# A three-operation bit join cut to two: where the weights' low three bits are made, and which engine subtracts in the MLP's first block

## The chip, the core and the metric

The kernel is one program on one core of a Trainium2 chip. The core's engines are PE (TensorE, matrix products), DVE (VectorE), ACT (ScalarE), POOL (GpSimd) and SP (SyncE, which here only starts transfers). The metric is the device time of one launch in microseconds.

## The reference

Three layers follow each other; all results are float32.

```python
# 1. linear attention: q, k, v of (4, 8, 576, 64), w_phi of (64, 128)
proj = x @ w_phi; proj -= max|proj|; phi = [exp(proj), exp(-proj)]
kv = sum_s k_p[s] v[s];  z = sum_s k_p[s];  out = (q_p @ kv) / (q_p @ z + 1e-6)
# 2. MLP: 2304 tokens, 512 wide, 1536 hidden
xn = x / rms(x) * rms_g
y = (silu(xn @ w_gate) * (xn @ w_val)) @ w_out
# 3. soft mixture of 8 experts with 4 slots each
logits = y @ phi; d = softmax over tokens; c = softmax over slots
out = c @ (relu((d.T @ y) @ w1) @ w2)
```

The three MLP weights arrive as 64-bit floats. The kernel has to turn them into 32-bit floats itself, from the two 32-bit words of each number.

## The kernel before

The first stage (0 to 136 us) works through the keys in 18 tiles of 128 tokens. Per tile, PE makes two projections `P` (L392), one for each half of the heads, in a PSUM buffer each; DVE takes the largest absolute value `mx` (L396) and subtracts it, giving `pr` (L400); ACT makes two exponentials `kp` (L413, L414) for each half; PE adds up the sums over tokens `kacc` (L437, L446). Beside this runs the attention of the first 384 queries: projections `P` (L320), `qmx` and `qpr` on DVE (L323, L324), transposes `T` and their exponentials `e` (L335, L337), then for each of four pairs of heads the products `num` and `den` (L204, L212), a reciprocal on DVE (L217), eight small copies on ACT (L222) and a product `xraw` on DVE (L223). The PSUM buffers of `num`, `den`, `T` and L320's `P` are three in all, taken in turn.

The second stage is the MLP in six blocks of 384 tokens. Block 0 runs from 136 to 232 us. For each of 12 pieces `m` of 128 hidden units PE multiplies 12 times for the gate `pg` and 12 times for the value `pv` (both L795) and 9 times for the output `acc` (L820 to L822). Between them stand ACT's tanh `t` (L802), two DVE products (L803, L807), ACT's rounded copy `hh` (L101) and the remainder `hl` = t - hh (L104). L822 reads `hl`. In block 0 the attention of the next 384 queries is spread over the same steps.

The weights are converted in 18 pieces of 128 x 1024 numbers, nine in the first stage (one per two tiles) and nine in block 0 (one per `m`). A piece goes through: a transfer into `wraw` (L122, 1 MB); ACT's scaling of the high word, as a float, into `wt` (L126); three DVE operations on the bits of `wt` in place (L133 shifts left by 3, L135 joins the sign, L137 joins the upper three bits of the low word); ACT's rounded copy into the weight tile (L101); POOL's remainder (L104, the "parts"). `wraw` has three buffers in the first stage and two in block 0; a new transfer into one waits until the last join of the old piece has read it. `wt` has two buffers in turn, free after POOL's parts.

The pieces of conversion are called at fixed steps of the loops (`conv_join` and others), but the order on each engine is then set by a scheduler of the language, which has its own estimates of durations. So the order in the trace is not that of the code, and a change of one operation moves others. Each engine works through its queue in order: an instruction that waits holds everything behind it.

Of the kernel before, what the change touches and what calls it, by code (L numbers as in the profile page):

```python
# [10 lines left out]
AF = mybir.ActivationFunctionType  # L11
ALU = mybir.AluOpType
# [12 lines left out]
MF = DFF // 128  # L25
NJ = MF // 2
NPRE = 9
KCONV, MCONV = (3, 2), (2, 1)
NX = 3
NLEFT = 2  # L30
# [33 lines left out]
def tile_kernel(ctx: ExitStack, tc: tile.TileContext, q2T, qT, kT, v, wbd, wg, wv, wo, rmsg, phi, w1, w2, consts, out):  # L64
# [47 lines left out]
    class Conv:  # L112
# [11 lines left out]
        def scale(self):  # L124
            self.w = self.wp.tile([128, 1024], F32, tag="S", name="wt", bufs=self.bufs[1])
            ACT.activation(out=self.w, in_=self.raw[:, :, 1].bitcast(F32), func=AF.Copy, scale=2.0 ** -112)  # L126

        def join(self):

            n = self.n = self.n + 1  # L130
            w, hi, lo = self.w.bitcast(U32), self.raw[:, :, 1], self.raw[:, :, 0]
            if n == 1:
                DVE.tensor_scalar(out=w, in0=w, scalar1=3, scalar2=None, op0=ALU.logical_shift_left)  # L133
            elif n == 2:
                DVE.scalar_tensor_tensor(out=w, in0=hi, scalar=0x80000000, in1=w, op0=ALU.bitwise_and, op1=ALU.bitwise_or)  # L135
            else:
                DVE.scalar_tensor_tensor(out=w, in0=lo, scalar=29, in1=w, op0=ALU.logical_shift_right, op1=ALU.bitwise_or)  # L137

        def parts(self):
            j, nm = self.key  # L140
# [19 lines left out]
    def conv_join():  # L160
        if convs:
            convs[-1].join()
            if convs[-1].n == 3:
                joined.append(convs.pop())

    def conv_parts():
# [201 lines left out]
    with ExitStack() as pk:  # L368
# [148 lines left out]
        for i in range(TILES):  # L517
            k, kn = ks[i], ks[i + 1] if i + 1 < TILES else None
            if i + 3 < TILES:
                ks[i + 3].load()  # L520
            if i + 2 < TILES:
                ks[i + 2].load_v()
            if i % 2 and i // 2 + 2 < NPRE:
                conv_load(sp, KCONV, sp)
            parts = batch_parts(i)
            b = parts[0][0]
            ends = i * 128 + parts[0][2] == (b + 1) * SEQ

            def finish():
                ev = Evac(b)  # L530
                fillers.extend([lambda n=n: ev.turn(n) for n in range(3)])

            if len(parts) > 1:
                k.kv(parts[0])
                finish()
            if kn:
                kn.project()
                kn.largest(0)
                if i % 2 == 0:
                    conv_join()  # L540
                kn.less(0)
                kn.largest(1)
                conv_join()
                kn.less(1)
            k.kv(parts[-1])
            for hf in range(2):
                if kn:
                    kn.exps(hf)
                if hf == 0 and i % 2:
                    conv_parts()  # L550
                    conv_scale()
                if fillers:
                    fillers.pop(0)()
                for f in qsteps[2 * i + hf]:
                    f()
            if ends and len(parts) == 1:
                finish()
# [46 lines left out]
    with ExitStack() as p2:  # L604
# [201 lines left out]
        def val(m, xs, t):  # L806
            DVE.tensor_tensor(out=t, in0=t, in1=wide("v", m, xs), op=ALU.mult)  # L807

        def split_h(t, early=False):
            hh = mp.tile([128, BLK], F32R, tag="hh", name="hh", bufs=1)  # L810
            hl = mp.tile([128, BLK], F32R, tag="hl", name="hl", bufs=1)
            split(hh, hl, t, hi_eng=ACT, lo_eng=POOL if early else DVE)
            return hh, hl

        def out_tile(m, hs, acc, i):
# [9 lines left out]
        xs = split_block(xraw.pop(0))  # L825
        t = gate(0, xs)
        val(0, xs, t)
        hs = split_h(t, True)
        steps = []
        q = Turned(q1p, ps, 1, {"misc": 3, "raw": 2, "pr": 4, "e": 1})  # L830
        q.begin()
# [3 lines left out]
        for blk in range(NBLK):  # L835
            acc = [ps.tile([128, DM], F32, tag=f"acc{i}", name=f"acc{i}", bufs=1) for i in range(TPB)]
            qsteps, qnext = qnext or [], None
            if blk == 1:
                tctx.close()
                q1ctx.close()  # L840
                qp = pool(qctx, "qp", side="right")
                q = Reduced(qp, ps, 2, {"misc": 3})
                q.begin()
                qsteps = q.steps()
                sp = pool(pctx, "post", side="right")
                S_run = stp.tile([128, 2 * DM], F32, tag="S", name="S_run", bufs=1)[0:96, 0:DM]
            if blk == NBLK - 1:
                pctx.close()
                qctx.close()
                kl = pool(ctx, "kl", side="right")  # L850
                xw = pool(ctx, "xw", bufs=NX, side="right")
                upool[:0] = [xw] * NX
                sp = pool(pctx, "post", side="right")
            if blk:
                x2 = []
                for i in range(TPB):
                    y = sp.tile([128, DM], F32, tag="x2", name="x2", bufs=TPB)
                    ACT.activation(out=y, in_=acc_done[i], func=AF.Copy, scale=0.5)
                    x2.append(y)
                steps = post(blk - 1, x2)  # L860
            plan = [[] for _ in range(3 * MF + 1)]
            for n, f in qsteps:
                plan[n].append(f)
            for n, f in zip(PSLOTS, steps):
                plan[n].append(f)
            done = [0]

            def fill():
                done[0] += 1
                if blk == 0:  # L870
                    n = (done[0] - 1) % CEVERY
                    if n == 0:
                        conv_parts()
                        conv_scale()
                    conv_join()
                    if n == 2:
                        conv_load(sp, MCONV, sp, stp)
                for f in plan[done[0] - 1]:
                    f()

            for m in range(MF):
                if m + 1 == MF and blk + 1 < NBLK:
                    xs = split_block(xraw.pop(blk + 1))
                more = m + 1 < MF or blk + 1 < NBLK
                if more:
                    t = gate((m + 1) % MF, xs)
                fill()
                if more:
                    val((m + 1) % MF, xs, t)
                fill()  # L890
                if more:
                    for i in range(TPB):
                        out_tile(m, hs, acc, i)
                if more:
                    hs = split_h(t, blk == 0 and m < MF - 3)
                fill()
                if blk == NBLK - 1 and m % 2 == 1:
                    unit(min(len(units) + (NX + 2 if m == 1 else 2), 17 + NX))
                if m == MF - 3 and 3 <= blk + 2 < NBLK:
                    q = Reduced(qp, ps, blk + 2, {"misc": 3})  # L900
                    q.begin()
                    qnext = q.steps()
            acc_done = acc
# [157 lines left out]
```

## Time and profile before

| | |
|---|---|
| median of 3 runs | 755.49 us (755.3 to 758.66) |
| the profiled execution | 756.4 us, of which the span from first to last instruction is 754.5 us |
| PE busy | 720.1 us (95%) |
| DVE busy | 444.4 us (59%) |
| ACT busy | 353.4 us (47%) |
| POOL busy | 121.2 us (16%) |
| mean granted TensorE clock | 0.987 |

The shares are means over stages with different limits. In 40 slices of 18.9 us each, DVE is busy for 5, 8, 9, 7, 9, 6, 9, 9, 8 and 4 tenths in the first ten (to 189 us), and about 5 tenths in the blocks that follow; PE has 7 to 9 tenths in the first ten and 9 afterwards. Everything the change touches lies before 232 us.

### The profile page before, as it was taken

What the parts mean: (1) busy time and instruction counts of PE and PEld (TensorE: products, weight loads), DVE (VectorE), ACT (ScalarE), POOL (GpSimd) and SP (SyncE); (2) the same over time, 40 slices, a digit from 0 to 9 for tenths busy, and PEclk for the clock granted to TensorE, in tenths of its full rate; (3) what the DMA queues carried; (4) which work ended last, traced back from release to release, by engine and by line L of the source; (5) the groups of instructions that cost most, each with busy time, mean ns of one, the idle gap of its engine ahead of it and who ended that gap; (6) DMA issues with size and microseconds to landing.
All of it is one profiled execution on the core that took longest, in us unless ns stands there. A gap on an engine that the chain in (4) does not pass through costs nothing.

```text
span 754.5 us, 12364 instructions
## 1 busy us (share of the span) xinstructions
PE 720.1 (95%) x4919; PEld 577.8 (77%) x4919; DVE 444.4 (59%) x816; ACT 353.4 (47%) x787; POOL 121.2 (16%) x70
## 2 busy tenths in 40 slices
PE   7998998997999999999999999999999999999994
PEld 4554555876788888898888988889888899988343
DVE  5897967699846556455565555645556453333313
ACT  5658765455644556434564346643465331212102
POOL 0222210245510211012110121101211010000000
PEclk9998999999999999999999999999999999999997
DMA  8664211544101100101000010000100046567798
GB/s 311 233 233 168 84 44 45 188 152 156 56 15 62 38 23 22 47 1 32 22 22 20 1 32 22 23 18 1 32 1 2 9 168 242 204 235 282 280 374 315
DMA packets 25145, 79.45 MB, mean 105 GB/s; under 512 B 2688, under 2 KB 13376, under 8 KB 18688
## 3 DMA queue, kind: packets, MB, share of 16 engines
q1 hardware_dynamic: 24864, 77.79, 29.5%
q10 hardware_dynamic: 224, 0.88, 0.4%
q8 instruction: 38, 0.62, 0.3%
q14 instruction: 19, 0.16, 0.1%
HBM read 71.99 MB, written 6.67 MB: 104 GB/s over the span
## 4 chain that ended last, share of the span: by engine, by line
PE 75%; DVE 11%; DMA 5%; ACT 5%; issue 2%; POOL 0%; SPq 0%; ACTq 0%; DVEq 0%
PE pv L795 18%; PE pg L795 17%; PE acc L820 6%; PE acc L821 6%; PE acc L822 6%; PE num L204 4%; PE kacc L437 3%; DMA eu<-in_w_dram 2%; DVE wt L135 2%; PE P L392 2%; PE den L212 2%; DVE wt L137 2%; PE kacc L446 2%; DMA wraw<-in_wg_dram 2%; ACT e L222 1%
## 5 line engine op out<-in xcount | busy, mean ns | idle before, releaser
L795 PE MATMUL pv<-xnh,wv 128*128 128x384 f32 x576 | 151.5, 344 | 1.1 <-DVE t L807 1.1
L795 PE MATMUL pg<-xnh,wg 128*128 128x384 f32 x576 | 150.1, 342 | 0.2 <-ACT xnh L101 0.2
L795 PEld LDWEIGHTS pv<-xnh,wv 128*128 128x128 f32 x576 | 103.1, 188 | 8.6 <-issue 6.7
L795 PEld LDWEIGHTS pg<-xnh,wg 128*128 128x128 f32 x576 | 104.7, 188 | 5.9 <-ACT xnh L101 0.6
L795 PE MATMUL pv<-xnl,wv 128*128 128x384 f32 x288 | 97.7, 339 | 0.0
L795 PE MATMUL pg<-xnl,wg 128*128 128x384 f32 x288 | 97.5, 338 | 0.0
L278 POOL PARTITION_ALL_REDUCE qe<-qe x32 | 50.0, 1562 | 247.3 <-ACT qe L277 227.7
L820 PE MATMUL acc<-wo,hh 128*128 128x512 f32 x216 | 88.4, 409 | 1.0 <-ACT hh L101 0.9
L822 PE MATMUL acc<-wo,hl 128*128 128x512 f32 x216 | 85.5, 396 | 1.9 <-POOL hl L104 1.9
L821 PE MATMUL acc<-wo,hh 128*128 128x512 f32 x216 | 85.8, 397 | 0.0
L101 ACT CAST hh<-t 128x384 fp32r<-128x384 f32 x72 | 36.7, 510 | 85.6 <-PE acc L821 68.7
L803 DVE SCALAR_TENSOR_TENSOR t<-t,pg 128x384 f32<-128x384 f32 x72 | 39.7, 551 | 52.6 <-ACT t L802 52.5
L802 ACT ACTIVATE t<-pg 128x384 f32<-128x384 f32 x72 | 35.1, 487 | 63.2 <-PE pg L795 63.2
L104 DVE TENSOR_TENSOR hl<-t,hh 128x384 fp32r<-128x384 f32 x62 | 34.5, 557 | 48.0 <-ACT hh L101 45.5
L222 ACT COPY qe<-qe 32x192 f32<-32x192 f32 x128 | 44.8, 350 | 31.7 <-DVE qe L217 30.4
L807 DVE TENSOR_TENSOR t<-t,pv 128x384 f32<-128x384 f32 x72 | 39.7, 552 | 30.2 <-PE pv L795 28.9
L795 PEld LDWEIGHTS pg<-xnl,wg 128*128 128x128 f32 x288 | 54.0, 188 | 0.3 <-DVE xnl L104 0.3
L795 PEld LDWEIGHTS pv<-xnl,wv 128*128 128x128 f32 x288 | 54.0, 188 | 0.1
L822 PEld LDWEIGHTS acc<-wo,hl 128*128 128x128 f32 x216 | 40.6, 188 | 12.5 <-POOL hl L104 2.7
L437 PE MATMUL kacc<-kp,vt 128*64 128x256 f32 (+1 forms) x320 | 44.1, 400 | 4.0 <-ACT kp L414 4.0
L820 PEld LDWEIGHTS acc<-wo,hh 128*128 128x128 f32 x216 | 40.7, 189 | 9.2 <-ACT hh L101 2.0
L821 PEld LDWEIGHTS acc<-wo,hh 128*128 128x128 f32 x216 | 40.7, 188 | 6.4
(188 smaller groups left out, 1091.0 us busy)
## 6 DMA issues: line engine op xcount, KB each, us to landing
eu<-in_w_dram SPq DMA_DIRECT2D x32, 1024.0 KB, 6.2
wraw<-in_wg_dram SPq DMA_DIRECT2D x6, 1024.0 KB, 6.0
wraw<-in_wv_dram SPq DMA_DIRECT2D x6, 1024.0 KB, 6.3
wraw<-in_wo_dram SPq DMA_DIRECT2D x6, 1024.0 KB, 4.9
qraw<-in_qT_dram SPq DMA_DIRECT2D x32, 192.0 KB, 2.3
raw<-in_kT_dram SPq DMA_DIRECT2D x18, 256.0 KB, 4.0
vt<-in_v_dram SPq DMA_DIRECT2D x18, 256.0 KB, 3.2
out_dram<-ob SPq DMA_DIRECT2D x18, 256.0 KB, 3.4
```

What stands on the lines that cost most here:

```text
L101: ACT.copy(out=hi, in_=src)
L104: (lo_eng or POOL).tensor_tensor(out=lo, in0=src, in1=hi.bitcast(F32), op=ALU.subtract)
L222: ACT.copy(out=rd[64 * hh + 32 * r:64 * hh + 32 * r + 32, g], in_=dn[o:o + 32])
L278: POOL.partition_all_reduce(e[:, 0], e[:, 1], channels=128, reduce_op=bass_isa.ReduceOp.absmax)
L437: PE.matmul(out=kva[o0:o0 + 64, hh // 2], lhsT=self.vt[r0:r1, h], rhs=kp[r0:r1, hh].rearrange("p s f -> p (s f)"), start=first and hh < 2, ...
L795: PE.matmul(out=p, lhsT=w[:, a, c], rhs=x, start=n == 0, stop=n == 11)
L802: ACT.activation(out=t, in_=g, func=AF.Tanh, scale=0.5)
L803: DVE.scalar_tensor_tensor(out=t, in0=t, scalar=1.0, in1=g, op0=ALU.add, op1=ALU.mult)
L807: DVE.tensor_tensor(out=t, in0=t, in1=wide("v", m, xs), op=ALU.mult)
L820: PE.matmul(out=acc[i], lhsT=hh[:, s], rhs=w[:, 0], start=m == 0, stop=False)
L821: PE.matmul(out=acc[i], lhsT=hh[:, s], rhs=w[:, 1], start=False, stop=False)
L822: PE.matmul(out=acc[i], lhsT=hl[:, s], rhs=w[:, 0], start=False, stop=m == MF - 1)
```

## The change

There are two parts. In the conversion, ACT gets a second operation per piece: it multiplies the low word, read as an unsigned integer, by 0.93 / 2^29 and writes it back as an integer in place, which leaves the three bits that are wanted (0 to 7, rounded). DVE's shift (L133) and one join are then a single operation, `(wt << 3) | lo`, and the sign join stays: two DVE operations for three. In block 0, `hl` for the first ten `m` moves from POOL to DVE, where it is made for all others already.

```diff
+LOW = 0.93 * 2.0 ** -29
...
             ACT.activation(out=self.w, in_=self.raw[:, :, 1].bitcast(F32), func=AF.Copy, scale=2.0 ** -112)
+            lo = self.raw[:, :, 0]
+            ACT.activation(out=lo, in_=lo, func=AF.Copy, scale=LOW)
...
             if n == 1:
-                DVE.tensor_scalar(out=w, in0=w, scalar1=3, scalar2=None, op0=ALU.logical_shift_left)
-            elif n == 2:
+                DVE.scalar_tensor_tensor(out=w, in0=w, scalar=3, in1=lo, op0=ALU.logical_shift_left, op1=ALU.bitwise_or)
+            else:
                 DVE.scalar_tensor_tensor(out=w, in0=hi, scalar=0x80000000, in1=w, op0=ALU.bitwise_and, op1=ALU.bitwise_or)
-            else:
-                DVE.scalar_tensor_tensor(out=w, in0=lo, scalar=29, in1=w, op0=ALU.logical_shift_right, op1=ALU.bitwise_or)
...
-            if convs[-1].n == 3:
+            if convs[-1].n == 2:
...
-                kn.largest(0)
-                if i % 2 == 0:
-                    conv_join()
-                kn.less(0)
+                kn.shift(0)
...
-            split(hh, hl, t, hi_eng=ACT, lo_eng=POOL if early else DVE)
+            split(hh, hl, t, hi_eng=ACT, lo_eng=DVE)
...
                         conv_scale()
-                    conv_join()
+                    else:
+                        conv_join()
```

In the changed file the two joins are L137 and L139, the scaling is L127, the new operation on the low word is L129, and later lines are one or two up. The changed kernel's instructions keep their order on PE but for some splits of `P` and `kacc` in the first stage; DVE and ACT are reordered up to 220 us, and on SP one load of queries and one of weights move up by a place.

The first place is DVE at the fifth piece (`wt_680`, `wraw_479`, the second value piece), between two key tiles. Before:

```order
L323 TENSOR_REDUCE qmx_539<-P_537 128x2
L133 TENSOR_SCALAR wt_680<-wt_680 128x1024
L324 TENSOR_TENSOR qpr_540<-P_537,qmx_539 128x256
L135 SCALAR_TENSOR_TENSOR wt_680<-wraw_479,wt_680 128x1024
L396 TENSOR_REDUCE mx_567<-P_557 128x4
L396 TENSOR_REDUCE mx_572<-P_558 128x4
L400 TENSOR_TENSOR pr_570<-P_557,mx_567 128x512
L400 TENSOR_TENSOR pr_575<-P_558,mx_572 128x512
L137 SCALAR_TENSOR_TENSOR wt_680<-wraw_479,wt_680 128x1024
```

Now, on the same engine at the same place:

```order
L325 TENSOR_REDUCE qmx_540<-P_538 128x2
L137 SCALAR_TENSOR_TENSOR wt_680<-wt_680,wraw_479 128x1024
L326 TENSOR_TENSOR qpr_541<-P_538,qmx_540 128x256
L398 TENSOR_REDUCE mx_568<-P_558 128x4
L398 TENSOR_REDUCE mx_572<-P_559 128x4
L402 TENSOR_TENSOR pr_570<-P_558,mx_568 128x512
L402 TENSOR_TENSOR pr_575<-P_559,mx_572 128x512
L139 SCALAR_TENSOR_TENSOR wt_680<-wraw_479,wt_680 128x1024
```

The first join stands where the shift stood, and nothing of the conversion is left between `qpr` and `mx`.

The second place is ACT a little later, ahead of the eight copies L222 (`wv1` is the weight tile of the fifth piece; `wraw_799` and `wt_1009` are the seventh; `wo1` and `wt_845` the sixth). Before:

```order
L214 COPY xraw_596<-num_597 128x384
L414 ACTIVATE kp_630<-pr_575 128x4x128
L337 ACTIVATE e2_531<-T_625 128x2x128 x2
L101 CAST wv1_842<-wt_680 128x1024
L126 ACTIVATE wt_1009<-wraw_799 128x1024
L222 COPY e2_298<-e2_298 32x192 x8
```

Now:

```order
L216 COPY xraw_596<-num_597 128x384
L102 CAST wv1_842<-wt_680 128x1024
L339 ACTIVATE e2_532<-T_625 128x2x128 x2
L129 ACTIVATE wraw_799<-wraw_799 128x1024
L102 CAST wo1_1006<-wt_845 128x1024
L224 COPY e2_298<-e2_298 32x192 x8
```

The scaling of the seventh piece, which needs the buffer that POOL's parts of the fifth piece free, has gone behind the copies; the new low-word operation and the sixth piece's rounded copy stand there instead.

The third place is ACT in block 0, about the exponentials `e` of `T_1835`, which PE's `num_1855` reads (`wt_1999`, `wraw_1901` are block 0's seventh piece). Before:

```order
L101 CAST hh_1801<-t_1754 128x384
L337 ACTIVATE e2_1786<-T_1808 128x2x128 x2
L126 ACTIVATE wt_1999<-wraw_1901 128x1024
L101 CAST wo4_1996<-wt_1928 128x1024
L802 ACTIVATE t_1826<-pg_1813 128x384
L337 ACTIVATE e2_1786<-T_1835 128x2x128 x2
```

Now:

```order
L102 CAST hh_1801<-t_1754 128x384
L339 ACTIVATE e2_1786<-T_1808 128x2x128 x2
L102 CAST wv4_1925<-wt_1832 128x1024
L801 ACTIVATE t_1826<-pg_1813 128x384
L339 ACTIVATE e2_1786<-T_1835 128x2x128 x2
L102 CAST wo4_1996<-wt_1928 128x1024
L127 ACTIVATE wt_1999<-wraw_1901 128x1024
L129 ACTIVATE wraw_1901<-wraw_1901 128x1024
```

The scaling of the seventh piece stood ahead of the tanh and these exponentials; now it stands behind both.

## Rows read from the trace of the kernel before

**Rows 1.** Busy us and instructions by stage: PE, PEld, DVE, ACT, POOL; PEclk, DMA, GB/s.
```profile
0.00:136.00 136.00, 122.64 (x1130) 72.31 (x1130) 105.49 (x174) 89.47 (x179) 21.47 (x13) 0.97 0.46 155
136.00:232.00 96.00, 88.52 (x533) 75.39 (x534) 74.15 (x93) 51.03 (x107) 36.95 (x19) 1.00 0.35 121
232.00:754.50 522.50, 508.90 (x3257) 430.13 (x3255) 264.76 (x550) 212.90 (x503) 62.78 (x38) 0.99 0.26 90
```

**Rows 2.** Groups by line, 0 to 290 us: busy us, mean ns | idle before.
```profile
L135 DVE SCALAR_TENSOR_TENSOR wt<-wraw,wt 128x1024 uint32<-128x1024 uint32 x18 | 27.6, 1534 | 0.2
...
L133 DVE TENSOR_SCALAR wt<-wt 128x1024 uint32<-128x1024 uint32 x18 | 22.6, 1258 | 6.9 <-ACT wt L126 6.9
...
L126 ACT ACTIVATE wt<-wraw 128x1024 f32<-128x1024 f32 x18 | 20.9, 1161 | 14.7 <-DMA wraw<-in_wg_dram 6.9 <-POOL wv L104 3.4 <-DMA wraw<-in_wv_dram 2.6
...
L104 POOL TENSOR_TENSOR hl<-t,hh 128x384 fp32r<-128x384 f32 x10 | 13.8, 1378 | 55.8 <-ACT hh L101 46.8 <-PE P L320 6.9 <-issue 2.0
...
L323 DVE TENSOR_REDUCE qmx<-P 128x2 f32<-128x256 f32 x24 | 9.8, 413 | 2.5 <-PE P L320 2.4
...
L101 ACT CAST wg<-wt 128x1024 fp32r<-128x1024 f32 x6 | 6.3, 1051 | 10.9 <-DVE wt L137 10.9
...
L104 DVE TENSOR_TENSOR hl<-t,hh 128x384 fp32r<-128x384 f32 x8 | 4.5, 558 | 4.9 <-ACT hh L101 4.8
```

**Rows 3.** The instructions of L133: shortest, median, longest in ns.
```profile
L133 DVE TENSOR_SCALAR wt<-wt x18: 680/694/2696, 14.3 to 196.9; 128x1024 uint32<-128x1024 uint32 x18
```

**Rows 4.** DVE and POOL in order of time, at three places: start us, us.
```profile
48.87 0.69 DVE L133 TENSOR_SCALAR wt<-wt 128x1024 uint32<-128x1024 uint32 x1
...
49.80 3.42 DVE L135 SCALAR_TENSOR_TENSOR wt<-wraw,wt 128x1024 uint32<-128x1024 uint32 x1
...
55.53 1.21 DVE L137 SCALAR_TENSOR_TENSOR wt<-wraw,wt 128x1024 uint32<-128x1024 uint32 x1
...
164.13 2.95 DVE L137 SCALAR_TENSOR_TENSOR wt<-wraw,wt 128x1024 uint32<-128x1024 uint32 x1
...
194.50 1.35 DVE L223 TENSOR_TENSOR xraw<-xraw,e 128x384 f32<-128x384 f32 x1
...
49.77 2.37 POOL L104 TENSOR_TENSOR wg<-wt,wg 128x1024 fp32r<-128x1024 f32 x1 [9.41 <-ACT wg L101]
```

**Rows 5.** The chain of waits from 49.8 to 67 us: start us, us, what.
```profile
58.16 0.95 ACT wv L101
...
59.18 2.38 POOL wv L104
...
61.58 1.17 ACT wt L126
...
65.53 0.56 DVE xraw L223
```

**Rows 6.** PE in order of time, 62 to 74 us.
```profile
62.82 0.71 PE L392 MATMUL P<-wbd_f,raw 64*128 64x128 f32 x6
66.58 1.19 PE L320 MATMUL P<-wbd_f,qraw 128*128 128x256 f32 x2 [3.05 <-DVE qpr L324]
```

**Rows 7.** Busy us by stretch of the first stage, columns as in rows 1.
```profile
14.00:50.00 36.00, 35.25 (x307) 20.45 (x304) 33.10 (x50) 23.41 (x42) 7.31 (x4) 1.00 0.74 257
...
66.00:80.00 14.00, 13.43 (x102) 8.23 (x103) 11.31 (x21) 13.21 (x29) 2.35 (x1) 0.76 0.35 119
```

**Rows 8.** PE's waits from 136 to 232 us: total us, times, longest.
```profile
PE num L204 <- ACT e L337: 2.7, 1, 2.7
PE acc L822 <- POOL hl L104: 1.9, 2, 1.1
PE pv L795 <- DVE t L807: 1.1, 1, 1.1
```

**Rows 9.** The chain of waits from 174 to 186 us.
```profile
175.11 6.10 DMA wraw<-in_wg_dram
...
181.29 1.16 ACT wt L126
```

More of the change, by code (lines that the diff above doesn't have):

```diff
@@ L807, in val, with split_h @@
             DVE.tensor_tensor(out=t, in0=t, in1=wide("v", m, xs), op=ALU.mult)
-        def split_h(t, early=False):
+        def split_h(t):
             hh = mp.tile([128, BLK], F32R, tag="hh", name="hh", bufs=1)
             hl = mp.tile([128, BLK], F32R, tag="hl", name="hl", bufs=1)
-            split(hh, hl, t, hi_eng=ACT, lo_eng=POOL if early else DVE)
+            split(hh, hl, t, hi_eng=ACT, lo_eng=DVE)
             return hh, hl
@@ L827, in tile_kernel @@
         val(0, xs, t)
-        hs = split_h(t, True)
+        hs = split_h(t)
         steps = []
@@ L894, in tile_kernel @@
                 if more:
-                    hs = split_h(t, blk == 0 and m < MF - 3)
+                    hs = split_h(t)
                 fill()
```

## The prediction

> **What bounds the kernel now.** I read the busy time by stage first. From 232 us on PE is busy 508.9 of 522.5 us [rows 1], and nothing of the change lies there, so all that can move is in the first 232 us. In the first stage no engine is full: PE 122.6, DVE 105.5, ACT 89.5 of 136 us; in block 0 PE has 88.5, DVE 74.2, ACT 51.0 of 96 us [rows 1]. PE therefore has 7.5 us to gain in block 0, and some 13 us in the first stage, part of it the start. What holds PE there is the order of short waits, so next I read PE's waits, and for the longest the chain that leads to it.
>
> The longest wait of the first stage is 3.05 us ahead of L320's projection at 66.58 us [rows 6]. After it the clock is granted at 0.76 in the mean from 66 to 80 us [rows 7]; between the levels 2.4 GHz (1.0) and 1.2 GHz (0.5) that is 0.24 / 0.5 x 14 = 6.7 us at the low one, in which half, 3.4 us, is lost. The chain back from this wait: DVE's xraw at 65.53 waits for eight copies on ACT, these stand behind the scaling L126 at 61.58, and that waits for POOL's parts from 59.18 to 61.55, which wait for the rounded copy that began at 58.16 [rows 5]. Before it stands the join L135 at 49.80 us, which took 3.42 us because POOL's parts had started 0.03 us earlier [rows 4]; alone such a join takes 1.21 (that at 55.53 in the same rows). In block 0 PE waits once 2.7 us for exponentials, twice, 1.9 us together, for `hl` from POOL, and once 1.1 us for a product on DVE [rows 8].
>
> **The change part by part.** DVE loses 18 shifts. Busy they come to 22.6 us [rows 2], but alone one takes 0.68, so 18 x 0.68 = 12.2 us are their own and 10.4 us were spent locked out by POOL [rows 3]. It gains ten `hl` at 0.558 = 5.6 us [rows 2]. POOL loses the ten, 13.8 us. ACT gains 18 operations over 1024 integers that the trace doesn't show. The nearest rows are the dense rounded copy, 1.05 us, and the scaling, which reads every second word, 1.16 us [rows 2]. Writing every second word too may cost the difference once more: 1.27. If integers took two passes it would be 2.3. I take 1.2, near the scaling, so 21.6 us in all, half of it in each stage. The new join has the operands of the old ones, two SBUF inputs of which one is strided; between 1.2 (alone) and 3.4 us (behind parts) [rows 4] I take the old ones' 1.21 where nothing locks it.
>
> The place near 50 us. With the shift gone the fifth piece's first join stands ahead of `qpr`, about 0.9 us earlier than L135 did, hence before POOL's parts start; POOL then waits and DVE does not. That saves 3.42 - 1.21 = 2.2 us. The shift's own 0.6 us I leave out, because PE's projections may not be there sooner. Further down the same chain the scaling has gone from ahead of the eight copies; with it go the wait for POOL (59.11 to 61.56, 2.45 us) and its own 1.17 us. In their place stand the low-word operation, 1.2, and a rounded copy, 1.05, and on DVE one `qmx` more ahead of `qpr`, 0.4 at most [rows 2, 5]. The chain gets 3.62 - 2.65 = 1.0 shorter. Together L320's projection comes 3.2 us earlier, at 63.4 us. PE gains less, since the six matmuls of the key projection that stand ahead of the wait (0.7 us) [rows 6] now stand behind it: 2.5 us. The wait that is left, 63.4 less 62.8 or some 0.6 us, is shorter than the 2.7 us in block 0 [rows 8] after which the clock stayed at 1.00 [rows 1]. So I count the 3.4 us of low clock as saved.
>
> What is late next is ACT. From 66 to 80 us it is busy 13.21 of 14 us [rows 7], and at the end of that stretch the new order puts two low-word operations ahead of a tile's exponentials: 2 x 1.2 = 2.4 us, all charged. From 14 to 50 us I count nothing, since PE is busy 35.25 of 36 us [rows 7]; the freed DVE time could be worth up to 1.5 us there, as PE's busy time holds short waits between split projections. After 80 us I count nothing either (0 to 1.5 us: one locked-out shift). First stage: 2.5 + 3.4 - 2.4 = 3.5 us.
>
> Block 0. The 2.7 us wait: ACT's scaling of the seventh piece stood ahead of the exponentials and waited for its transfer, issued at 175.11 and landed at 181.21 [rows 9]. In the new order it stands behind them, with its low-word operation. The transfer itself comes no earlier, but nobody on PE waits for it at once; all 2.7 us go. The 1.1 us wait: the third join at 164.13 took 2.95 us behind POOL's parts [rows 4], with the product PE needed queued behind it on DVE. There is now one join fewer for this piece ahead of that product: 1.1 us go. The two waits for `hl`: on DVE it takes 0.56 instead of 1.38 us [rows 2], but stands in a queue behind joins; I take half, 0.9 us (0 to 1.9). Against this nine low-word operations on ACT, each with tanh or `hh` queued behind it and PE waiting for those in turn. ACT has 45 us free in 96 [rows 1], so I put one in nine on the path: 1.2 us (0 to 5). A transfer into a buffer still waits for the last join, now the second; the chain of a piece changes by one ACT operation, +1.2, and one shift, -0.7, with nothing else behind it on SP in block 0. Block 0: 2.7 + 1.1 + 0.9 - 1.2 = 3.5 us.
>
> The sum is 3.5 + 3.5 = 7.0 us. The profiled execution took 756.4 us (its span of 754.5 and 1.9 around it), so it would take 749.4. It lies 0.9 above the median of 755.49; for the median I predict 748.5 us.
>
> A rule speaks against the second part. L223, with two inputs in SBUF, took 1.35 us behind POOL at 194.50 [rows 4], and 0.56 otherwise [rows 5]. `hl` has such inputs as well. The Trainium skill (SBUF — State Buffer, Who interferes with whom) says that a VectorE operation with two SBUF inputs and a GpSimd operation that reads SBUF lock each other out for the whole instruction, and that issue order decides who waits. The trace agrees: 3.42 against 1.21 us.
>
> **The rivals.** First, `hl` locked out. POOL's nine parts in block 0 at some 2.4 us [rows 4] hold the lock for 22 of 96 us; of ten `hl` 2.3 would meet one, and an average rest of 1.2 us makes 2.8 us. If PE waits for all of it, block 0 gives 3.5 - 2.8 = 0.7, and the time is 755.5 - 3.5 - 0.7 = 751.3. For it speaks row 194.50, against it that only two of ten slower `hl` on POOL made PE wait.
>
> Second, the gain of the first stage is hidden anyway. If PE's order rather than DVE's load sets the pace (PE 35.25 of 36 us before 50), and the eight copies still end so late that PE idles over 2.7 us at 63, the clock still falls. Then 2.5 + 3.4 are gone, ACT's 2.4 is paid only where PE idles, and block 0 alone counts, itself with the half of its terms: 755.5 - 1.8 = 753.7.
>
> Third, slower: ACT becomes the bound of the first stage. Its place is between 40 and 90 us, where three conversion operations in a row now stand ahead of a tile's exponentials. Nine low-word operations at 1.2 are 10.8 us; if all of that is on the path while the 3.2 us before 66 and block 0's 3.5 are still won, the time is 755.5 + 10.8 - 6.7 = 759.6, and with integers at 2.3 us about 10 more. It decides once a low-word operation takes longer than the 0.8 us that ACT has free from 66 to 80 [rows 7] and no slack ahead of `kp` takes up the rest. Against it: over the stage ACT has 46 us free [rows 1].
>
> **How the numbers follow.** My forecast has 0.60, `hl` locked out 0.11, hidden 0.16, slower 0.13. About 0.5% (3.8 us) is what a measurement can tell from no change: below 751.7 is faster, above 759.3 slower. The forecast lies below 751.7 in nearly all of its chance, the first rival in half, the second in a little: faster 0.62. Slower has 0.09 of the third rival's 0.13, and the rest, 0.29, is the same. The lower end comes from the open bounds: 1.5 before 50, 1.5 after 80, 2.4 not paid on ACT: 748.5 - 5.4 = 743.1. The upper end leaves out the worse part of the third rival: 757.5. The forecast's own range is 743.1 to 751.7.
>
> **What would show it.** Right: the first join near 50 us takes 1.2 us and POOL's parts there more than 2.4; no wait of about 3 us ahead of L320's projection and a granted clock near 1.00 from 66 to 80; in block 0 no wait of `num` for exponentials, and PE's busy time unchanged in a stage shorter by 3 to 4 us. The low-word operation reads 1.1 to 1.3 us. Wrong: that operation at 2 us or more; a low clock at another place of the first stage; `kp` or `hh` on ACT as what PE waits for; `hl` on DVE over 1 us with PE waiting.

## The result, and the profile after

The changed kernel takes 746.71 us (median of 4 runs, 745.82 to 748.41) against 757.08 for the kernel before (4 runs); the ratio is 0.9854, with a 95% interval of 0.9816 to 0.9892. Six later runs gave 747.68 and a ratio of 0.9858 (0.9828 to 0.9889). Its profiled execution took 745.82 us with a span of 743.8: 10.7 us less than the span of the one before.

The windows by stage answer to [rows 1], with the same columns, cut at the first gate matmul of block 0, at that of block 1, and at the first `x2tp`, where the end part begins; first the changed kernel, then the end part of the kernel before.

```profile
0.00:133.70 133.70, 120.52 (x1130) 70.00 (x1130) 97.83 (x165) 97.65 (x188) 22.47 (x13) 0.99 0.46 158
133.70:223.30 89.60, 86.71 (x534) 76.16 (x535) 65.73 (x95) 60.61 (x116) 23.03 (x9) 1.00 0.37 129
223.30:687.20 463.90, 462.08 (x2764) 406.68 (x2763) 246.86 (x503) 203.04 (x477) 60.01 (x36) 1.00 0.18 61
687.20:743.80 56.60, 45.24 (x493) 23.17 (x491) 17.69 (x47) 9.95 (x26) 2.75 (x2) 0.92 0.90 327
```

```profile
696.10:754.50 58.40, 46.51 (x493) 23.23 (x491) 17.55 (x47) 9.87 (x26) 2.76 (x2) 0.89 0.88 317
```

The kernel before had the same cuts at 136.1, 232.2 and 696.1. So the first stage gave 2.4 us, block 0 6.5, blocks 1 to 5 nothing (463.9 in both), and the end part, which the change doesn't touch, 1.9. DVE's busy time in block 0 fell from 74 to 66 us while ACT's rose from 51 to 61.

The groups of the first 290 us answer to [rows 2]; behind them the low-word operation alone, with its shortest, median and longest in ns.

```profile
L139 DVE SCALAR_TENSOR_TENSOR wt<-wraw,wt 128x1024 uint32<-128x1024 uint32 x18 | 27.4, 1519 | 0.0
L137 DVE SCALAR_TENSOR_TENSOR wt<-wt,wraw 128x1024 uint32<-128x1024 uint32 x18 | 26.7, 1481 | 7.1 <-ACT wraw L129 6.6 <-issue 0.5
...
L129 ACT ACTIVATE wraw<-wraw 128x1024 uint32<-128x1024 uint32 x18 | 20.7, 1159 | 0.7 <-DMA wraw<-in_wo_dram 0.7
L105 DVE TENSOR_TENSOR hl<-t,hh 128x384 fp32r<-128x384 f32 x19 | 11.8, 620 | 10.7 <-ACT hh L102 10.6
```

```profile
L129 ACT ACTIVATE wraw<-wraw x18: 1127/1152/1226, 13.2 to 188.2; 128x1024 uint32<-128x1024 uint32 x18
```

The operation I had to price takes 1.15 us. The joins still average 1.5 us where one that meets nothing takes 1.22: 54.1 - 36 x 1.22 = 10.2 us go on waiting for GpSimd.

The place near 50 us, which answers to [rows 4]: DVE, POOL, then PE a little later, in order of time.

```profile
48.32 1.22 DVE L137 SCALAR_TENSOR_TENSOR wt<-wt,wraw 128x1024 uint32<-128x1024 uint32 x1
```

```profile
49.21 2.54 POOL L105 TENSOR_TENSOR wg<-wt,wg 128x1024 fp32r<-128x1024 f32 x1 [9.97 <-ACT wg L102]
```

```profile
63.23 0.67 PE L322 MATMUL P<-wbd_f,qraw 128*128 128x256 f32 x2 [0.88 <-DVE qpr L326]
...
116.58 3.43 PE L439 MATMUL kacc<-kp,vt 128*64 128x256 f32 x16
```

The join that took 3.42 us now stands ahead of GpSimd's parts and takes 1.22. The projection that waited 3.05 us until 66.58 [rows 6] starts at 63.23 after 0.88. The second PE row is new: sixteen matmuls that take 1.95 us at the full clock took 3.43. The granted clock (the third number from the end) in the stretch of [rows 7] and in the new one:

```profile
66.00:80.00 14.00, 11.66 (x121) 7.12 (x116) 11.50 (x20) 13.91 (x30) 0.00 (x0) 1.00 0.29 95
110.00:120.00 10.00, 9.51 (x81) 5.67 (x82) 8.14 (x25) 6.33 (x16) 0.00 (x0) 0.84 0.22 82
```

Before 80 us PE waits twice for exponentials that stand behind ACT's two low-word operations (2.27 us from 74.09):

```profile
77.44 1.08 PE L439 MATMUL kacc<-kp,vt 128*64 128x256 f32 x8 [0.82 <-ACT kp L416]
79.29 1.08 PE L439 MATMUL kacc<-kp,vt 128*64 128x256 f32 x8 [0.77 <-ACT kp L416]
```

PE's waits in block 0, as in [rows 8]:

```profile
PE num L206 <- ACT e L339: 1.2, 1, 1.2
PE pg L794 <- DVE t L802: 1.0, 1, 1.0
PE ssq L241 <- DVE s L232: 0.7, 1, 0.7
```

The long wait for exponentials is gone, and so are those for `hl` and for the product of the value matmuls. The waits of 1.2 us, for the exponentials of a later `num`, and of 1.0 us, for the product of the gate, are new. The `num` of the long wait before and now, then the later one:

```profile
184.08 0.87 PE L204 MATMUL num<-e,kv 128*64 128x192 f32 x8 [2.67 <-ACT e L337]
```

```profile
174.17 1.52 PE L206 MATMUL num<-e,kv 128*64 128x192 f32 x16
...
196.67 0.87 PE L206 MATMUL num<-e,kv 128*64 128x192 f32 x8 [1.20 <-ACT e L339]
```

Ahead of the later one stands a join at 192.30 us that takes 2.95 us beside GpSimd's parts; ACT's rounded copy waits for it, with the exponentials behind.

### The profile page after: what moved, and what is told of

Same layout as the page of the kernel before. It is cut to its first block, busy times and chain, and to the rows that moved or that the text cites. A ratio compares the mean times of both kernels' runs of the same rounds, so it can differ in the third digit from the quotient of the medians.

```text
span 743.8 us, 12360 instructions
## 1 busy us (share of the span) xinstructions
PE 714.6 (96%) x4919; PEld 576.0 (77%) x4919; DVE 428.1 (58%) x808; ACT 371.2 (50%) x805; POOL 108.3 (15%) x60
## 4 chain that ended last, share of the span: by engine, by line
PE 73%; ACT 10%; DVE 6%; DMA 5%; issue 2%; POOL 1%; SPq 0%; ACTq 0%; DVEq 0%; POOLq 0%
PE pv L794 18%; PE pg L794 17%; PE acc L819 6%; PE acc L820 6%; PE acc L821 6%; PE num L206 4%; PE kacc L439 3%; DMA eu<-in_w_dram 2%; PE den L214 2%; ACT e L224 2%; PE kacc L448 2%; DVE wt L137 1%; DMA wraw<-in_wg_dram 1%; ACT wt L127 1%; PE P L394 1%
## 5 line engine op out<-in xcount | busy, mean ns | idle before, releaser
L105 DVE TENSOR_TENSOR hl<-t,hh 128x384 fp32r<-128x384 f32 x72 | 41.3, 574 | 53.7 <-ACT hh L102 51.2
L794 PEld LDWEIGHTS pv<-xnl,wv 128*128 128x128 f32 x288 | 54.1, 188 | 0.1
```

Of the source, the lines that this page charges most:

```text
L105: (lo_eng or POOL).tensor_tensor(out=lo, in0=src, in1=hi.bitcast(F32), op=ALU.subtract)
L794: PE.matmul(out=p, lhsT=w[:, a, c], rhs=x, start=n == 0, stop=n == 11)
```

## The experiments

Twelve runs. The table has the place of the three cuts in each profile, as lengths in us, and the median of the runs. The kernel before had medians of 757.9, 758.8 and 757.6 us beside the three groups of runs.

| kernel | first stage | block 0 | blocks 1 to 5 | end part | median | ratio to before (95%) |
|---|---|---|---|---|---|---|
| before | 136.1 | 96.1 | 463.8 | 58.4 | 757.08 | |
| changed | 133.7 | 89.6 | 463.9 | 56.6 | 746.71 | 0.9854 (0.9816 to 0.9892) |
| e1 joins only | 134.2 | 93.3 | 463.8 | 57.2 | 750.75 | 0.9908 (0.9880 to 0.9936) |
| e2 hl only | 140.8 | 93.2 | 463.8 | 59.8 | 758.57 | 1.0004 (0.9974 to 1.0035) |
| e2 again, one run | 137.2 | 93.5 | 463.8 | 58.5 | 754.81 | |
| e3 no low-word operation | 129.0 | 95.1 | 463.8 | 56.6 | 745.69 | 0.9845 (0.9807 to 0.9884) |
| e5 a third DVE operation | 135.3 | 96.4 | 463.7 | 57.6 | 756.11 | 0.9981 (0.9958 to 1.0004) |
| e4 third buffer | 133.8 | 89.3 | 463.7 | 57.1 | 745.98 | 0.9852 (0.9797 to 0.9906) |
| e6 parts write only | 134.6 | 86.7 | 463.7 | 56.3 | 743.09 | 0.9801 (0.9758 to 0.9843) |
| e7 low word twice | 135.8 | 89.0 | 463.7 | 56.7 | 746.47 | 0.9858 (0.9810 to 0.9906) |
| e8 query path first | 133.7 | 90.1 | 463.9 | 58.1 | 747.26 | 0.9859 (0.9815 to 0.9902) |
| e9 quarters | 136.6 | 89.1 | 463.9 | 57.1 | 748.03 | 0.9852 (0.9824 to 0.9881) |
| e10 quarters, third buffer | 131.0 | 88.8 | 463.7 | 56.3 | 744.62 | 0.9808 (0.9782 to 0.9834) |
| changed, again | 133.8 | 89.4 | 463.9 | 56.2 | 747.68 | 0.9858 (0.9828 to 0.9889) |

The first stage's length holds a difference that is not the kernel's. The same eight matmuls near the start, in the changed kernel and in e4:

```profile
9.34 1.08 PE L439 MATMUL kacc<-kp,vt 128*64 128x256 f32 x8 [1.49 <-ACT kp L416]
```

```profile
9.37 1.97 PE L439 MATMUL kacc<-kp,vt 128*64 128x256 f32 x8 [1.41 <-ACT kp L416]
```

By 15 us PE is 1.4 to 1.9 us behind in e1, e2's first profile, e4, e6, e7 and e9, and less than 0.6 us in the others.

**One part at a time (e1, e2).** The joins alone; `hl` goes back to GpSimd:

```diff
-            split(hh, hl, t, hi_eng=ACT, lo_eng=DVE)
+            split(hh, hl, t, hi_eng=ACT, lo_eng=POOL if early else DVE)
```

> The two-operation join with ScalarE's low-word operation, but the values' lower parts of block 0 again by GpSimd. Theory (the join part carries the gain: less VectorE time and one lock collision less in the first stage, ScalarE's scaling out of PE's way in block 0): the first stage ends where the changed kernel's does, at 133.7 us (-2.4 against before), block 0 keeps some 4 of the 6.5 us it won, and the waits of PE for hl (1.9 us before) are back; 748 to 750 us against 746.7 for the whole change. Rival A (it is hl that made block 0 shorter): block 0 is as long as before, 752 to 754 us. Rival B (the two parts need each other, the gain is a lucky order): within 2 us of the kernel before.

The first stage, whose instructions stand in the changed kernel's order on every engine, is within 0.5 us of that kernel's (134.2), so the joins carry its gain. (It began 1.5 us late, and had no low clock at 116 us.) Block 0 wins 2.9 of 6.5 us. The waits for `hl` are not what is missing (0.4 us): PE waits for other things, through DVE. PE's waits, then DVE, POOL and the clock at the place:

```profile
PE pg L794 <- DVE t L802: 1.9, 1, 1.9
PE T L337 <- DVE qpr L326: 1.5, 1, 1.5
...
PE acc L821 <- POOL hl L105: 0.4, 1, 0.4
```

```profile
185.65 3.37 DVE L137 SCALAR_TENSOR_TENSOR wt<-wt,wraw 128x1024 uint32<-128x1024 uint32 x1
```

```profile
185.54 2.39 POOL L105 TENSOR_TENSOR wg<-wt,wg 128x1024 fp32r<-128x1024 f32 x1 [0.47 <-ACT wg L102]
```

```profile
190.00:195.00 5.00, 3.20 (x11) 0.66 0.00 0
```

The join began 0.1 us after the parts and waited them out, with `qpr` and the product behind it, and after PE's waits the clock is low (0.66 granted from 190 to 195 us). The parts had waited for ACT's copy, not for `hl`, and DVE and ACT have another order in this block than in the changed kernel; that this meeting comes from `hl` on GpSimd is not shown. The sum, 750.75, is at the upper edge of what I had expected.

The other part alone has the three joins of before, and `lo_eng=DVE` in every call:

> The three joins of before, no low-word operation on ScalarE; only the values' lower parts of block 0 by VectorE. Theory: the first stage is as before (ends at 136.1 us, with the 3.42 us join at 49.8 and the low clock from 66 to 80), block 0 wins the waits for hl and a little of GpSimd's lock, 1 to 3 us; 753 to 756 us. Rival A (hl carries block 0): block 0 6.5 us shorter, 749 to 751 us. Rival C (hl locked out behind GpSimd's parts with three joins in the queue): block 0 longer than before, 757 us or more.

> The kernel with only the values' lower parts on VectorE once more, one look. In its first profile the first stage, whose instructions stand in the order of the kernel before, ended at 140.8 us instead of 136.1, with the clock granted low between 107 and 117 us. Theory (whether the clock falls there is chance, and accounts for the spread of this kernel's times from 752.0 to 761.1 us): the first stage ends anywhere between 136 and 141 us, block 0 takes 93.2 +- 0.5 us. Rival (it comes with the change): 140.8 +- 0.5 us again.

Block 0 is 2.9 us shorter in one profile and 2.6 in the other, as the theory had it; rival A falls. With the joins' 2.9 that makes 5.5 to 5.8 of the 6.5 us: in block 0 the parts nearly add. But the whole, 758.57, is no faster than before. The reason stands in the first stage, whose instructions are, on every engine, in the order of the kernel before, and which took 140.8 and 137.2 us instead of 136.1. The same sixteen matmuls, in the kernel before, and in e2's first profile:

```profile
106.11 1.94 PE L437 MATMUL kacc<-kp,vt 64*64 64x256 f32 x16
```

```profile
107.60 2.82 PE L437 MATMUL kacc<-kp,vt 64*64 64x256 f32 x16
```

e2's second profile has them at 1.94 us again, and loses time at 120 us instead. The long wait near 65 us and the low clock behind it are there in all three (0.91 granted from 60 to 100 us); a fall after 100 us comes in some executions and not in others. The rival that it comes with the change falls by a first stage of 137.2. It doesn't explain all: e2's ten runs had a clock of 0.982 or less in six cases, none of the 21 runs of before beside them under 0.983. Why this kernel loses more of its clock stays open, and so does whether `hl` alone would gain anything in the median.

In e2 the three joins and shifts of before take 72.7 us on DVE (72.6 in the second profile), against 77.2 before (27.6 and 22.6 in [rows 2], and 27.0 for L137); the operations are the same, only GpSimd's ten `hl` are gone:

```profile
L135 DVE SCALAR_TENSOR_TENSOR wt<-wraw,wt 128x1024 uint32<-128x1024 uint32 x18 | 27.4, 1521 | 0.2
...
L137 DVE SCALAR_TENSOR_TENSOR wt<-wraw,wt 128x1024 uint32<-128x1024 uint32 x18 | 25.3, 1407 | 0.1
...
L133 DVE TENSOR_SCALAR wt<-wt 128x1024 uint32<-128x1024 uint32 x18 | 20.0, 1113 | 4.5 <-ACT wt L126 4.5
```

In the kernel before six of them met `hl` alone and took 3.7 us more than they do alone. The first, and the `hl` that it met:

```profile
143.49 1.92 DVE L135 SCALAR_TENSOR_TENSOR wt<-wraw,wt 128x1024 uint32<-128x1024 uint32 x1
```

```profile
143.20 1.13 POOL L104 TENSOR_TENSOR hl<-t,hh 128x384 fp32r<-128x384 f32 x1 [35.76 <-ACT hh L101]
```

With two joins the same step gives less: they take 55.2 us in e1 and 54.1 in the changed kernel. And PE's waits for `hl` are not what block 0 wins: in e2's second profile, with the block 2.6 us shorter, 1.6 of the 1.9 us are still there.

```profile
PE acc L822 <- DVE hl L104: 1.6, 2, 1.2
```

**The price of ScalarE's operation (e3, e7).** First without it, then twice:

```diff
-            ACT.activation(out=lo, in_=lo, func=AF.Copy, scale=LOW)
...
-  (...) scalar=3, in1=lo, op0=ALU.logical_shift_left, op1=ALU.bitwise_or)
+  (...) scalar=3, in1=lo, op0=ALU.logical_shift_left, op1=ALU.bitwise_and)
```

The AND with the raw low word spoils the whole weight and not only its lowest three bits, so e3 tells of the time alone.

> The changed kernel without ScalarE's low-word operation; the first join takes the unscaled word with an AND, so the weights' lowest three bits are left out. Theory (18 operations of 1.15 us cost 2.4 us ahead of kp at 74 us and about 1.2 us in block 0): 743 to 745 us, first stage ended by about 131 to 132.5 us. Rival D (ScalarE has the time everywhere, its operations cost nothing): 746 to 747.5 us. Rival E (ScalarE's operations are on the path throughout): below 740 us.

```diff
             ACT.activation(out=lo, in_=lo, func=AF.Copy, scale=LOW)
+            ACT.activation(out=lo, in_=lo, func=AF.Copy, scale=1.0)
```

> The changed kernel with ScalarE's low-word operation done twice (the second multiplies by 1), 18 x 1.15 = 20.7 us more on ScalarE, half of it in each stage. Without the operation the first stage ended at 129.0 us instead of 133.7, and block 0 took 5.5 us longer. Theory (ScalarE's queue sets the pace of the first stage, and joins that wait for ScalarE hold up VectorE's products in block 0): first stage 3 to 5 us longer, block 0 1 to 4 us longer; 750 to 756 us. Rival D (ScalarE has the time, 371 of 744 us busy): 746 to 748.5 us. Rival H (the first stage only took its gain from the clock, block 0 gives back what the first stage loses): 746 to 749 us with the two parts of opposite sign.

Neither moves the whole: 745.69 without, 746.47 with two, 746.71 with one. In both the scheduler also put PE, DVE and ACT in another order, so neither shows the price of the operation by itself. The theory of 750 us or more falls; of the rivals, H has the opposite signs right, but not the reason. Without the operation the first stage is 4.7 us shorter, 3.0 of them gained before 60 us (where I had counted nothing) with the clock at 1.00, and 1.0 because the changed kernel's low clock at 116 us is missing. With two it is 2.1 us longer: a wait of 2.30 us ahead of the projection at 65.18 (0.88 in the changed kernel), then a low clock (0.83 granted from 70 to 80 us). Block 0 doesn't pay for the second one (89.0), and without any it is 5.5 us longer. There the join, no longer held by the low word, starts inside GpSimd's parts. DVE, POOL, PE and, in the windows, PE's busy time with the clock behind its count, in e3:

```profile
182.51 3.08 DVE L136 SCALAR_TENSOR_TENSOR wt<-wt,wraw 128x1024 uint32<-128x1024 uint32 x1
```

```profile
182.02 2.49 POOL L105 TENSOR_TENSOR wv<-wt,wv 128x1024 fp32r<-128x1024 f32 x1 [3.92 <-ACT wv L102]
```

```profile
186.06 0.49 PE L336 MATMUL T<-cst,qpr 128*128 128x128 f32 x2 [1.86 <-DVE qpr L325]
```

```profile
185.00:190.00 5.00, 3.26 (x11) 0.63 0.00 0
190.00:195.00 5.00, 5.00 (x23) 0.69 0.01 3
```

PE waits 1.86 us for `qpr` behind that join, and the clock is low until about 193. So an operation of ACT seems to be worth what it does to the meeting of DVE and GpSimd, more than its own 1.15 us; since the order changed as well, that is argued and not shown.

**DVE's time put back (e5).**

```diff
             if n == 1:
+                DVE.tensor_scalar(out=w, in0=w, scalar1=0, scalar2=None, op0=ALU.logical_shift_left)
```

> The changed kernel with an empty shift by 0 of each piece put ahead of its first join on VectorE: VectorE's time is back (18 x 0.68 us and its lock collisions), ScalarE keeps the low-word operations, and the order is the changed kernel's. Theory (VectorE's time and its collisions with GpSimd carry the first stage, the place of the scaling carries most of block 0): first stage ends at 136 us or later, block 0 1 to 2 us longer than in the changed kernel; 749 to 753 us. Rival B (the new order carries it, VectorE's time is slack): 746 to 748 us.

756.11 us: 9.4 of the 10.4 us are gone again (1.8 are left against the kernel before beside it), above the range of the theory. But the order is not the changed kernel's, though I had expected that: with the shifts the scheduler moved other operations of DVE and ACT too, in both stages. So e5 does not decide between DVE's time and the order, and rival B is not excluded by it. The eighteen shifts take 13.5 us. The first stage is 1.6 us longer than the changed kernel's (135.3; I had 136 or more); block 0 is 6.8 us longer, more than three times what I expected, nearly all of it one kind of wait:

```profile
PE pg L795 <- DVE t L803: 6.1, 3, 3.4
```

The longest of them, on DVE, POOL and PE:

```profile
204.53 2.43 DVE L105 TENSOR_TENSOR hl<-t,hh 128x384 fp32r<-128x384 f32 x1 [1.07 <-ACT hh L102]
```

```profile
204.15 2.39 POOL L105 TENSOR_TENSOR wo<-wt,wo 128x1024 fp32r<-128x1024 f32 x1 [2.24 <-ACT wo L102]
```

```profile
212.74 0.72 PE L795 MATMUL pg<-xnh,wg 128*128 128x384 f32 x2 [3.40 <-DVE t L803]
```

Here `hl` itself is locked out, 2.43 us beside the parts; a reciprocal on DVE, the eight copies and the tanh on ACT and the product `t` that PE needs follow it one after the other. This is the first rival of the prediction, with PE waiting. That the kernel is as slow in block 0 as the one before, though `hl` stays on DVE, has this as one cause; the rest I did not take apart.

**The lock (e6).** GpSimd fills its output with 0 instead of subtracting (the weights' remainders are left out):

```diff
-            split(u[:, 0], u[:, 1], self.w, hi_eng=ACT, lo_eng=POOL)
+            ACT.copy(out=u[:, 0], in_=self.w)
+            POOL.memset(u[:, 1].bitcast(F32), 0.0)
```

> The changed kernel with GpSimd's parts (two inputs read from SBUF) replaced by a fill with 0 of the same output, so the weights' remainders are left out; VectorE's joins then find no GpSimd operation that reads beside them. Theory of the lock: all 36 joins take about 1.2 us (53.8 us together in the changed kernel, 43.6 without collisions), hl 0.55 throughout, VectorE has 10 to 11 us less. Of that PE can gain only what it still waits for: 3.1 us in block 0 and 2 to 3 in the first stage; 741 to 745 us. Rival F (VectorE's time is worth what the added shift cost, 9.3 us for 13.5 us of it): 739 to 740 us. Rival G (no lock; slow joins come from the transfers or their own operands): joins as slow as before, 746 to 748 us.

```profile
L137 DVE SCALAR_TENSOR_TENSOR wt<-wt,wraw x18: 1209/1224/1244, 16.2 to 189.2; 128x1024 uint32<-128x1024 uint32 x18
```

All joins take 1.21 to 1.25 us, where the changed kernel's went up to 3.28: rival G falls. But the fills need no weights and ran ahead of them, nine before 9 us and nine between 141 and 150 us, so that only three joins met one. One of these, and its fill:

```profile
142.77 1.23 DVE L137 SCALAR_TENSOR_TENSOR wt<-wt,wraw 128x1024 uint32<-128x1024 uint32 x1 [0.53 <-ACT wraw L129]
```

```profile
142.35 0.96 POOL L145 MEMSET wv<- 128x1024 f32 x1
```

So e6 takes GpSimd out of the way altogether, as a lock and as what holds the buffers `wt`. Block 0 is 2.9 us shorter: 2.2 of its 3.1 us of waits are gone, and 0.7 of PE's busy time. 743.09 lies in the theory's range. The first stage kept its length: 1.5 us late at the start, PE was 0.7 us ahead of the changed kernel from 93 to 114 us and lost clock again (0.83 from 110 to 120 us, 0.91 to 140). The Trainium skill (SBUF — State Buffer, Who interferes with whom) says that a VectorE instruction with two SBUF inputs contends with a GpSimd instruction that reads SBUF, not with one that only writes. The trace agrees, as far as three joins go: beside fills they took 1.22 to 1.23 us.

**Order and buffers (e4, e8).** A third buffer for the scaled weights in the first stage, and the query path's steps ahead of the conversion in block 0:

```diff
-KCONV, MCONV = (3, 2), (2, 1)
+KCONV, MCONV = (3, 3), (2, 1)
```

> The changed kernel with a third buffer for the scaled weights in the first stage, so that ScalarE's scaling no longer waits for GpSimd's parts (in the changed kernel 1.06 us at 51.8 and 1.12 us at 82.9, with the exponentials queued behind). Theory (ScalarE's queue sets when PE gets kp, and PE waits for kp 3.8 us in that stage): the first stage ends 1 to 2 us earlier, the rest is unchanged; 744.5 to 746.5 us against 746.7. Rival (PE's order or VectorE sets the pace there; the freed time only moves the wait): first stage within 0.5 us of 133.7; 746 to 748 us.

```diff
+                for f in plan[done[0] - 1]:
+                    f()
                 if blk == 0:
                     n = (done[0] - 1) % CEVERY
...
-                for f in plan[done[0] - 1]:
-                    f()
```

> The changed kernel with the order in block 0 turned: in each slot the query path's steps first, the conversion (scaling, low word, join, parts) behind them. Theory (what PE still waits for in block 0, 1.2 us for exponentials and 1.0 us for a product on VectorE, stands behind the conversion in the queues): block 0 is 1 to 2.5 us shorter, the first stage unchanged; 744 to 746 us. Rival I (the conversion is then later, the product of the next tile stands behind a join that waits for the low word): block 0 as long or up to 3 us longer; 746.5 to 750 us.

Both leave the time where it is (745.98 and 747.26). e4's first stage ends at 133.8 as the rival had it, but not for its reason: its PE was 1.6 us later at 60 us already, won 0.5 from there to 114, and had no low clock at 116 (1.00 from 110 to 120), worth 1.0. e8 tests nothing: the turned code came out of the scheduler with the changed kernel's instructions in the changed kernel's order on all five engines. It is one more profile of that kernel, and the 0.5 us by which its block 0 is longer are the spread of one program, not rival I.

**A shorter lock (e9, e10).** GpSimd's parts in four operations, and these with the third buffer:

```diff
-            split(u[:, 0], u[:, 1], self.w, hi_eng=ACT, lo_eng=POOL)
+            ACT.copy(out=u[:, 0], in_=self.w)
+            for c in range(0, 1024, 256):
+                s = slice(c, c + 256)
+                POOL.tensor_tensor(out=u[:, 1, s], in0=self.w[:, s], in1=u[:, 0, s].bitcast(F32), op=ALU.subtract)
```

> The changed kernel with each of GpSimd's parts (2.4 us) done in four operations of a quarter of the columns; the result is the same. Theory (a VectorE operation that meets GpSimd's waits for the end of that one operation, so a quarter is a shorter wait): the joins' surplus over 1.22 us each (9.9 us in the changed kernel) falls to some 3 us, GpSimd's parts take 3 to 5 us instead of 2.4, and the kernel wins most of the 3.6 us that it won without GpSimd's reads; 743.5 to 745.5 us. Rival J (the two engines now take turns, the parts end later, and ScalarE's scaling waits for the buffer): 746 to 749 us. Rival K (VectorE waits for the whole of the parts all the same): joins as before, 746 to 747 us.

> The changed kernel with GpSimd's parts in quarters and the third buffer for the scaled weights in the first stage, so that parts which end later hold up nothing on ScalarE there. Theory: as with quarters alone, or up to 1 us better where the parts end later; 743 to 745.5 us. Rival J: 746 us or more.

In both the joins wait for a quarter only; in e10 one of the two joins, and a kind of part:

```profile
L137 DVE SCALAR_TENSOR_TENSOR wt<-wt,wraw x18: 1203/1226/1809, 15.2 to 188.6; 128x1024 uint32<-128x1024 uint32 x18
```

```profile
L147 POOL TENSOR_TENSOR wg<-wt,wg x24: 721/741/1725, 20.0 to 183.9; 128x256 fp32r<-128x256 f32 x24
```

The longest join is 1.81 us instead of 3.28, and rival K falls. The parts now take some 3 us and more, and there e9 runs into rival J: ACT's scaling waits 10.3 us for them, against 3.4 in the changed kernel. e10 has 4.7. (Of e9's longer first stage, 1.9 us come from the start.) The scaling in e9, then in e10:

```profile
L127 ACT ACTIVATE wt<-wraw 128x1024 f32<-128x1024 f32 x18 | 20.8, 1158 | 13.4 <-POOL wg L147 6.4 <-POOL wv L147 3.9 <-DMA wraw<-in_wg_dram 2.2
```

```profile
L127 ACT ACTIVATE wt<-wraw 128x1024 f32<-128x1024 f32 x18 | 21.0, 1168 | 7.5 <-POOL wv L147 3.0 <-DMA wraw<-in_wg_dram 1.8 <-POOL wg L147 1.7
```

With both edits the kernel takes 744.62 us, 3.1 less than the changed kernel beside it (747.68); the two intervals overlap a little. In the profile, which is that of its fastest run, 2.7 us of it lie in the first stage (1.6 between 60 and 111 us, 1.0 of clock at 116) and 0.6 in block 0. It is the fastest version here with the full result.

**The end part.** The changed kernel once more:

> The changed kernel once more, for a second profile and for times beside those of the two kernels above on the same chip. Theory (what the change gives lies in the first stage and block 0; the 1.9 us at the end are TensorE's clock in that execution): 746 to 747.5 us, first stage ends between 133 and 134.5 us, block 0 takes 89.6 +- 0.5 us, and the time from the first x2tp to the end lies anywhere between 56.3 and 59.8 us, as in the other kernels. Rival (the end became shorter by the change): 56.6 +- 0.2 us again.

First stage and block 0 came as expected (133.8 and 89.4), the end part at 56.2, a little below the range. What decides is e8, which runs the changed kernel's instructions in their order, and whose end part took 58.1. The same stretch, the second eight us of the end part, in the changed kernel and in e8 (PE's busy time, then its clock):

```profile
695.24:703.24 8.00, 7.57 (x69) 1.00 0.71 230
```

```profile
695.65:703.65 8.00, 7.57 (x57) 0.79 0.54 201
```

The kernel before had 0.79 there too. So this stretch's clock goes either way with the same instructions, and the 1.9 us are not shown to be the change's. That the end part is mostly shorter where it begins earlier (56.3 us at 683.5, 59.8 at 697.8, but 56.2 at 687.1) I saw and did not test.

## Why the prediction was right, and where its terms were off

The direction and the range were right; the sum was 3.6 us too high (749.4 against 745.8 for the profiled executions). That it came so near is in part luck: the first stage gave 1.1 us less than forecast, block 0 3.0 more, and the end part 1.9 without a term. In detail:

- **The place near 50 us**: join 1.22 us, parts after it, projection at 63.23 where I had 63.4, clock 1.00 from 66 to 80. PE stood 5.3 us earlier at 74 us (a `kvt` part, 74.22 against 79.53), 0.55 of them gained before 60; the sum had 2.5 + 3.4 = 5.9.
- **ACT's charge behind it**: 2.4 us for two low-word operations ahead of `kp`; the lead fell from 5.3 to 3.4 us by 81 us (`kvt`, 81.31 against 84.74). It was 3.4 again at 113 us, so the place was right and the charge 1.9, most of it the two waits for `kp`.
- **After 80 us**, "0 to 1.5": here the first stage failed by its sign. A low clock at 116 us took 1.0 back (the last kvt part, 112.93 to 131.53, takes 18.6 us against 17.6 before), so that 2.4 of the predicted 3.5 were left. That low clock is in all three profiles of this program (e8 is the third), and not in e1, which has the same order there. I had listed "a low clock at another place" as a sign of error and given it no price.
- **Block 0, the joins**: 2.7 + 1.1 - 1.2 = 2.6 predicted, 2.9 in e1. The 2.7 and the 1.1 us went as forecast, but new waits of 1.2 and 1.0 us came, for which the sum had no term. What the low word costs on the path no run shows by itself; a second one made the block no longer (89.0 in e7, in another order).
- **Block 0, `hl`**: the term that was mis-sized. I took half of the waits named `hl`, 0.9 us; it measured 2.6 to 2.9 alone (e2) and 3.6 on top of the joins (changed kernel against e1, whose low clock after 190 us is part of it). I had counted `hl` as something PE waits for, and priced its lock only as a danger to itself on DVE. On GpSimd it was also a reader that locked DVE out: DVE's joins and shifts took 4.5 us less without it (e2). How the 3.6 us divide, with the joins only 1.1 us shorter there, stays open. The first rival (`hl` locked out) hardly happened in the changed kernel, where the slowest took DVE 1.87 us and PE never waited for it; in e5 it did.
- **PE's busy time in block 0** was to stay the same; it fell from 88.7 to 86.7 us. I take it that waits too short to be shown as idle time lay inside it, as I had said for the stretch before 50 us and not for this one. In e6 the same matmuls in the same order, also at a clock of 1.00, take 86.1 us; no run separates the single waits.
- **The end part**: no term, 1.9 us, the clock of that execution.

The second rival (hidden) needed a low clock at 66 us, which no profile of the changed kernel has. The third (ACT the bound) fell with e7: eighteen more operations of 1.16 us left the time at 746.47. What DVE's time is worth without a new order no run shows. The lock shows in every run: each slow join or shift overlaps an operation of GpSimd, and where none reads beside them (e6) none is slow.

## What to carry to other kernels

An operation that shares a lock is priced by what it keeps others from as well as by who waits for it: look for the slow instances of the engine on the other side (here the 3.4 us joins), not for its own name in the list of waits. Where two engines lock each other out instruction by instruction, shorter instructions can help, once the buffers allow the longer total (3.1 us here). Where a scheduler sets the order, compare the order of every variant before its time is read: a small edit can move much else (e3, e5, e7), or nothing at all (e8). And a kernel whose clock falls after a wait should be read in more than one profile: a gain of 3 us in one stage can be hidden by, or be nothing but, the clock.

## What the runs showed of the hardware that I had not expected

- ACT's copy of 1024 integers with a scale, in place, with every second word read and written, takes 1.15 us, the same as a scaling that only reads so (1.16): integers and the strided output cost nothing more.
- A fill by GpSimd of 128x1024 words took 0.95 us and slowed none of the three joins that met one; a subtraction of the same size took 2.4 and stretched joins to 3.3.
- Four GpSimd operations of 256 columns take 4 x 0.74 = 3.0 us by their median, against 2.4 for one of 1024.
- With the same instruction order the granted clock after 100 us stayed at 1.00 in one execution and was 0.66 from 107 to 117 us in another, worth 3.2 us at that place by the 1.5 us that the first stage was behind before it and the 4.7 after it.
